# First products of the third token tile as two halves of 256 columns

## The chip, the cores and the metric

The kernel runs on one core of a Trainium2 chip. The metric is the device time of one execution in microseconds; lower is better. Three runs of the kernel before took 572.45 to 573.59 us, median 572.46.

## The reference

A decaying linear attention (2 sequences, 8 heads, 768 positions, head dimension 64) gives 1536 tokens of 512 features. They pass through two feed-forward layers, each 512 to 2048 to 512, the first with Mish, the second with SiLU:

```
x = attention(q, k, v, lam).reshape(1536, 512)
h = x @ w_in              # 1536 x 2048
x = (h * tanh(softplus(h))) @ w_out
h = x @ w2_in
out = (h * sigmoid(h)) @ w2_out
```

All is in float32.

## The kernel before

TensorE multiplies in float32r, one pass over four-byte operands. To keep float32 precision each operand is split in a high and a low part (`xh` and `xl` of the activations, `wh` and `wl` of the weights, `gh` and `gl` behind the nonlinearity), and each product is made of three: high by high, low by high, high by low.

The 1536 tokens are three tiles of 512 (t = 0, 1, 2). The 2048 hidden features of each layer are 16 blocks of 128; over both layers that makes 32 blocks n = 0 to 31, in eight groups of four. Group 0 runs for all three tiles during and just behind the attention (the first 92 us or so). From group 1 on, tiles 0 and 1 are taken together: the class `Block` (line 516) makes their first products by seven products of half size instead of eight (tiles `a`, `b`, `c`, `e`). Tile 2 goes alone, through `emit_h` (line 390).

`emit_h(t, n)` makes one block of h for one token tile: a PSUM bank `ph` of 128 features by 512 tokens, into which 12 matmuls accumulate: 4 slices `kk` of the 512 input features, times the three pairs of parts. Each has its own 128x128 weights; a float32r matmul loads them itself, and the trace shows that as a LDWEIGHTS record (engine PEld) and a MATMUL record (PE). Then `activate` (line 376) has ScalarE apply the nonlinearity twice, to `gh` and in place to `ph`, and DVE makes `gl` from the two (line 377). `emit_o` (line 413) makes the second products from `gh`, `gl`: 12 matmuls of 512 columns into four banks `po`, which over the four blocks of a group accumulate; DVE adds them to `acc` at the group's end (line 437).

The order of the work is written by hand: a list of steps for each group, issued in that order on every engine. In groups 2 to 7 the tail of the list interleaves the four `emit_h` of tile 2 with four `emit_o` of tile 1:

```
tail = [hs[0], os[4], hs[1], os[5], hs[2], os[6], hs[3], os[7]]
```

`hs[f]` is `emit_h(2, n0 + f)`. In group 3 the last two `hs` come together behind the last `os`. The second products of tile 2 (`fills`) follow in the next group. ScalarE, DVE and GpSimd split the weights of later groups meanwhile, and SyncE issues their loads from DRAM.

Of the kernel before, what the change touches and what calls it, by code (L numbers as in the profile page):

```python
# [17 lines left out]
def decay_attention_mish_silu_kernel(  # L18
# [8 lines left out]
    nc = tc.nc  # L27
    P = 128
# [6 lines left out]
    T = 512  # L35
    NB = NT // T
    CPB = T // C
    KD = DM // P
    NF = w1.shape[0]
    GF = 4  # L40
# [138 lines left out]
    def x_tile(key):  # L179
        if key not in xs:  # L180
            h = xp.tile([P, KD, T], F32R, tag="xh", name="xh")
            l = xp.tile([P, KD, T], F32R, tag="xl", name="xl")
            xs[key] = (h, l)
        return xs[key]
# [167 lines left out]
    def bank(name):  # L352
        nbank[0] += 1
        if len(late) > 2 and nbank[0] % 2:
            return late[2].tile([P, T], F32, tag="x", name=name)
        return ps_h.tile([P, T], F32, tag="h", name=name)
# [14 lines left out]
    def activate(ps, mm, t, n):  # L371

        gh, gl = [gp.tile([P, T], F32R, tag=tag, name=tag) for tag in ("gh", "gl")]
        gts[n, t] = (gh, gl)
        for to in (gh, ps):
            nc.scalar.activation(to, ps, AF.Mish if mm == 0 else AF.Silu)  # L376
        later.append(lambda: nc.vector.tensor_tensor(out=gl, in0=ps, in1=gh.bitcast(F32), op=ALU.subtract))  # L377

    def emit_h(t, n, first=False):
        mm = n // NF  # L380
        xt = x_tile(t)
        assert (n, 0) in ready and not any(key[0] == t for key, _ in rest)
        wi = wtiles[n, 0]
        ph = bank("ph")
        i = 0

        lst = (0, 1) if first else (1, 0)
        early = [(0, 0), lst[::-1]]
        for wsel, xsel, kk in [(*e, kk) for kk in range(KD) for e in early] + [(*lst, kk) for kk in range(KD)]:
            nc.tensor.matmul(  # L390
                ph, lhsT=wi[wsel][:, kk * P : (kk + 1) * P], rhs=xt[xsel][:, kk, :],
                start=(i == 0), stop=(i == 3 * KD - 1),
            )
            i += 1
        activate(ph, mm, t, n)

    def emit_o(t, n, first, last):
# [211 lines left out]
    for i, (t, f) in enumerate(steps):  # L609
        n = i + PH  # L610
# [11 lines left out]
        if i < LAG or n >= N:  # L622
            run_split(2)
        emit_h(t, f, f == 0)
        if n < N:
            if i < LAG:
# [22 lines left out]
    for g in range(1, 2 * NG):  # L649
# [4 lines left out]
        os = [(0, 0), (0, 1), (0, 2), (0, 3), (1, 1), (1, 0), (1, 3), (1, 2)]  # L654
        os = [o(t, f, i % 4 == 0, i % 4 == 3) for i, (t, f) in enumerate(os)]
        hs = [lambda n=n0 + f: emit_h(2, n) for f in range(GF)]
        sp = lambda fn, *a: lambda: fn(*a)
        nxt = [[lambda p=p: split_pair(p)] if p < NF else [] for p in (pa + 2, pa + 3)]
# [111 lines left out]
```

## Time and profile before

| | us |
|---|---|
| median of three runs | 572.46 |
| lowest and highest | 572.45, 573.59 |
| profiled execution | 572.03 |
| its span, first to last instruction | 570.3 |
| TensorE matmuls busy | 559.8 |
| TensorE weight loads busy | 454.9 |
| VectorE (DVE) busy | 314.4 |
| ScalarE (ACT) busy | 286.9 |
| GpSimd (POOL) busy | 163.1 |

A matmul is recorded from its start to the end that the profiler models for it; consecutive matmuls overlap, so a row's duration is longer than the time from one start to the next. Weight loads have an engine name of their own (PEld) and run beside matmuls. The tile names in a row are `out<-in`; numbers of buffers are left out. The mean granted clock of TensorE over the span is 0.998.

### The profile page before, as it was taken

How to read it: one execution, taken by the hardware profiler on the slowest of the kernel's cores; microseconds unless marked ns; L12 is line 12 of the kernel's file. 1: busy time of each engine (PE TensorE's matmuls, PEld its weight loads, DVE VectorE, ACT ScalarE, POOL GpSimd, SP SyncE). 2: the span in 40 equal slices, each digit the busy share in tenths (PEclk: the TensorE clock that was granted, in tenths of full speed). 3: DMA queues.
4: the chain of work that ended last, by engine and by line, in shares of the span. 5: the costliest groups of instructions: out<-in, count | busy, mean ns of one | idle time of the engine just before them, and what ended most of it. 6: DMA issues, size and time to landing. Idle time of an engine off the chain costs nothing.

```text
span 570.3 us, 7604 instructions
## 1 busy us (share of the span) xinstructions
PE 559.8 (98%) x2960; PEld 454.9 (80%) x2960; DVE 314.4 (55%) x458; ACT 286.9 (50%) x537; POOL 163.1 (29%) x139
## 2 busy tenths in 40 slices
PE   8999999999999999999999999999999999999996
PEld 5777777887787788888887788888888888888885
DVE  3675635684556675536669974434734654455231
ACT  2666442655454573354656874546543654355210
POOL 2564430322115123122362643211312212302000
PEclk9999999999999999999999999999999999999999
DMA  7984610123022132212211132212310322100103
GB/s 238 423 305 160 278 39 1 38 74 111 0 76 74 38 110 75 74 36 76 81 68 37 38 117 68 74 38 74 111 61 15 100 85 68 45 0 1 74 28 121
DMA packets 14072, 50.30 MB, mean 88 GB/s; under 512 B 1488, under 2 KB 2512, under 8 KB 12756
## 3 DMA queue, kind: packets, MB, share of 16 engines
q1 hardware_dynamic: 14036, 49.82, 24.8%
q8 instruction: 23, 0.38, 0.3%
q14 instruction: 13, 0.11, 0.1%
HBM read 46.66 MB, written 3.15 MB: 87 GB/s over the span
## 4 chain that ended last, share of the span: by engine, by line
PE 88%; DVE 3%; DMA 3%; ACT 2%; issue 2%; POOL 1%; SPq 0%; DVEq 0%; POOLq 0%; ACTq 0%
PE po L413 44%; PE ph L390 18%; PE b L516 9%; PE a L516 6%; PE c L516 3%; PE e L516 3%; DMA xslot<-x 2%; PE px L333 1%; PE s L292 1%; PE px L326 1%; DVE acc L437 1%; PE pc L312 1%; DVE acc L427 1%; ACT gh L376 1%; POOL qd L281 0%
## 5 line engine op out<-in xcount | busy, mean ns | idle before, releaser
L170 POOL TENSOR_TENSOR wl<-dec,wh 128x512 fp32r<-128x512 f32 x64 | 85.4, 1336 | 279.1 <-ACT wh L169 222.1
L413 PE MATMUL po<-gh,wh 128*128 128x512 f32 x192 | 75.9, 395 | 0.1
L413 PE MATMUL po<-gh,wl 128*128 128x512 f32 x192 | 74.9, 390 | 0.1
L413 PE MATMUL po<-wh,gh 128*128 128x512 f32 x192 | 74.8, 389 | 0.0
L413 PE MATMUL po<-wl,gh 128*128 128x512 f32 x192 | 74.7, 389 | 0.0
L413 PE MATMUL po<-wh,gl 128*128 128x512 f32 x192 | 74.7, 389 | 0.0
L377 DVE TENSOR_TENSOR gl<-ph,gh 128x512 fp32r<-128x512 f32 x40 | 27.5, 688 | 72.0 <-ACT ph L376 72.0
L376 ACT ACTIVATE gh<-ph 128x512 fp32r<-128x512 f32 x40 | 23.9, 598 | 81.0 <-PE ph L390 80.8
L390 PE MATMUL ph<-xh,wh 128*128 128x512 f32 x160 | 63.2, 395 | 0.7 <-ACT xh L340 0.7
L390 PE MATMUL ph<-xl,wh 128*128 128x512 f32 x160 | 60.8, 389 | 0.0
L125 DVE SCALAR_TENSOR_TENSOR dec<-dec,slot 128x512 uint32<-128x512 uint32 x64 | 50.7, 793 | 16.9 <-ACT slot L98 16.9
L437 DVE TENSOR_TENSOR acc<-po,acc 128x512 f32<-128x512 f32 x72 | 45.7, 685 | 23.7 <-PE po L413 23.7
L169 ACT CAST wh<-dec 128x512 fp32r<-128x512 f32 x64 | 39.5, 618 | 37.7 <-DVE dec L129 37.2
L170 POOL TENSOR_TENSOR tl<-t,th 128x512 fp32r<-128x512 f32 x28 | 37.8, 1358 | 61.8 <-ACT th L169 58.4
L129 DVE SCALAR_TENSOR_TENSOR dec<-slot,dec 128x512 uint32<-128x512 uint32 x64 | 50.6, 790 | 1.7
L413 PE MATMUL po<-gl,wh 128*128 128x512 f32 x192 | 51.4, 389 | 0.0
L390 PE MATMUL ph<-xh,wl 128*128 128x512 f32 x160 | 44.4, 390 | 0.0
L413 PEld LDWEIGHTS po<-gh,wh 128*128 128x128 f32 x192 | 36.0, 188 | 9.6 <-DVE acc L437 1.4
L97 ACT ACTIVATE dec<-slot 128x512 f32<-128x512 f32 x64 | 42.7, 667 | 0.2 <-DMA slot<-w 0.2
L98 ACT ACTIVATE slot<-slot 128x512 uint32<-128x512 uint32 x64 | 42.6, 666 | 0.0
L413 PEld LDWEIGHTS po<-wh,gh 128*128 128x128 f32 x192 | 36.0, 188 | 7.8 <-issue 0.3
L413 PEld LDWEIGHTS po<-gh,wl 128*128 128x128 f32 x192 | 36.0, 188 | 7.7 <-POOL wl L170 0.6
(117 smaller groups left out, 949.4 us busy)
## 6 DMA issues: line engine op xcount, KB each, us to landing
slot<-w SPq DMA_DIRECT2D x64, 512.0 KB, 3.6
xslot<-x SPq DMA_DIRECT2D x10, 1024.0 KB, 8.8
out<-acc SPq DMA_DIRECT2D x12, 256.0 KB, 2.1
xslot<-x SPq DMA_DIRECT2D x4, 512.0 KB, 4.2
dmask<-scr SPq DMA_DIRECT2D x2, 256.0 KB, 4.7
pw<-lam SPq DMA_DIRECT2D x1, 0.0 KB
scr<-pw SPq DMA_DIRECT2D x1, 8.0 KB
```

Source lines behind the costliest of these rows:

```text
L97: nc.scalar.activation(decs[n, i].bitcast(F32), high.bitcast(F32), AF.Copy, scale=2.0**-112)
L98: nc.scalar.activation(low, low, AF.Copy, scale=TOP3, bias=2.0**-21 - 0.5)
L125: nc.vector.scalar_tensor_tensor(out=d, in0=d, scalar=3, in1=low, op0=ALU.logical_shift_left, op1=ALU.bitwise_or)
L129: nc.vector.scalar_tensor_tensor(out=d, in0=high, scalar=0x80000000, in1=d, op0=ALU.bitwise_and, op1=ALU.bitwise_or)
L169: nc.scalar.copy(hi, f)
L170: nc.gpsimd.tensor_tensor(out=lo, in0=f, in1=hi.bitcast(F32), op=ALU.subtract)
L376: nc.scalar.activation(to, ps, AF.Mish if mm == 0 else AF.Silu)
L377: later.append(lambda: nc.vector.tensor_tensor(out=gl, in0=ps, in1=gh.bitcast(F32), op=ALU.subtract))
L390: nc.tensor.matmul(ph, lhsT=wi[wsel][:, kk * P : (kk + 1) * P], rhs=xt[xsel][:, kk, :], start=(i == 0), stop=(i == 3 * KD - 1),)
L413: nc.tensor.matmul(po[t][j], lhsT=lhsT, rhs=rhs, start=(first and wsel + gsel == 0), stop=(last and gsel == 1))
L437: nc.vector.tensor_tensor(out=acc[:, j, :], in0=po[t][j], in1=acc[:, j, :], op=ALU.add)
L516: nc.tensor.matmul(self.b[dst], lhsT=w[ws][:, kk * P : (kk + 1) * P], rhs=x[xx][:, kk, :], start=(start and i == 0), stop=(i == 5), skip_g ...
```

## The change

For t = 2 and n >= 8 (groups 2 to 7, 24 calls of `emit_h`) the 12 matmuls of 512 columns become two rounds of 12 with 256 columns each, into the left and then the right half of the same bank. Only the first matmul of the first round carries the start flag, which marks the bank as empty; the first of the second round finds its columns unwritten and overwrites them. `activate` follows both rounds, as before. All other calls keep one round of 512 columns.

```
-        i = 0
-
         lst = (0, 1) if first else (1, 0)
         early = [(0, 0), lst[::-1]]
-        for wsel, xsel, kk in [(*e, kk) for kk in range(KD) for e in early] + [(*lst, kk) for kk in range(KD)]:
-            nc.tensor.matmul(
-                ph, lhsT=wi[wsel][:, kk * P : (kk + 1) * P], rhs=xt[xsel][:, kk, :],
-                start=(i == 0), stop=(i == 3 * KD - 1),
-            )
-            i += 1
+        order = [(*e, kk) for kk in range(KD) for e in early] + [(*lst, kk) for kk in range(KD)]
+        width = T // 2 if t == 2 and n >= 2 * GF else T
+        for c in range(0, T, width):
+            for i, (wsel, xsel, kk) in enumerate(order):
+                nc.tensor.matmul(
+                    ph[:, c : c + width], lhsT=wi[wsel][:, kk * P : (kk + 1) * P],
+                    rhs=xt[xsel][:, kk, c : c + width], start=(c == 0 and i == 0), stop=(i == 3 * KD - 1),
+                    skip_group_check=True,
+                )
         activate(ph, mm, t, n)
```

On TensorE, the end of the last of the 24 pieces and what follows it, before (`wh` and `wl` are the two parts of the weights, `x4` stands for four matmuls over `kk`; a row has the weight load in it):

```order
L390 MATMUL ph<-xh,wh_4152 128x512
L390 MATMUL ph<-xl,wh_4152 128x512
L390 MATMUL ph<-xh,wl_4153 128x512 x4
L413 MATMUL po<-wh_4347,gh 128x512
L413 MATMUL po<-wl_4348,gh 128x512
L413 MATMUL po<-wh_4347,gl 128x512
```

The same place of TensorE's order now, at the seam between the two rounds (the line numbers are one higher):

```order
L391 MATMUL ph<-xh,wh_4380 128x256
L391 MATMUL ph<-xl,wh_4380 128x256
L391 MATMUL ph<-xh,wl_4381 128x256 x4
L391 MATMUL ph<-xh,wh_4380 128x256
L391 MATMUL ph<-xl,wh_4380 128x256
L391 MATMUL ph<-xh,wh_4380 128x256
```

Where `po` came, the same weights now come a second time for the other 256 columns, 12 matmuls more, and `po` follows these. On ScalarE, DVE, GpSimd and SyncE the instructions stand in the same order in both programs.

## Rows read from the trace of the kernel before

**Rows 1.** The page: its head, TensorE's busy time, the chain by engine and line.

```profile
span 570.3 us, 7604 instructions
...
PE 559.8 (98%) x2960; PEld 454.9 (80%) x2960; DVE 314.4 (55%) x458; ACT 286.9 (50%) x537; POOL 163.1 (29%) x139
...
PE 88%; DVE 3%; DMA 3%; ACT 2%; issue 2%; POOL 1%; SPq 0%; DVEq 0%; POOLq 0%; ACTq 0%
PE po L413 44%; PE ph L390 18%; PE b L516 9%; PE a L516 6%; PE c L516 3%; PE e L516 3%; DMA xslot<-x 2%; PE px L333 1%; PE s L292 1%; PE px L326 1%; DVE acc L437 1%; PE pc L312 1%; DVE acc L427 1%; ACT gh L376 1%; POOL qd L281 0%
```

**Rows 2.** Busy time by stretch, bf16 start, groups 2 and 7; columns in the first row.

```profile
core 0: us, PE busy (x) PEld busy (x) DVE busy (x) ACT busy (x) POOL busy (x), PEclk, DMA share, GB/s
7.00:8.20 1.20, 1.20 (x8) 0.54 (x6) 0.00 (x0) 0.00 (x0) 0.00 (x0) 1.00 0.90 293
196.00:268.00 72.00, 71.81 (x317) 59.16 (x316) 41.06 (x61) 39.41 (x73) 19.74 (x15) 1.00 0.24 81
510.00:560.00 50.00, 50.00 (x221) 41.21 (x220) 18.36 (x29) 14.47 (x27) 4.23 (x3) 1.00 0.12 43
```

**Rows 3.** Groups by line and shape: count, busy us, mean ns, idle before.

```profile
L390 PE MATMUL ph<-xl,wh 128*128 128x512 f32 x160 | 60.8, 389 | 0.0
...
L390 PEld LDWEIGHTS ph<-xl,wh 128*128 128x128 f32 x160 | 30.0, 188 | 6.1
```

**Rows 4.** Timeline, TensorE matmuls of the last piece: start us, duration us, what.

```profile
548.76 0.39 PE L390 MATMUL ph<-xh,wh 128*128 128x512 f32 x1
548.99 0.39 PE L390 MATMUL ph<-xl,wh 128*128 128x512 f32 x1
...
551.48 0.39 PE L413 MATMUL po<-wh,gh 128*128 128x512 f32 x1
```

**Rows 5.** Timeline, weight loads of the same piece.

```profile
548.99 0.19 PEld L390 LDWEIGHTS ph<-xh,wh 128*128 128x128 f32 x1
```

**Rows 6.** Waits from 92 to 570 us: total us, times, longest.

```profile
ACT gh L376 <- PE ph L390: 70.2, 23, 7.1
...
PEld e L516 <- DVE gl L377: 2.1, 3, 0.9
PEld b L516 <- ACT b L535: 1.5, 2, 0.8
PEld po L413 <- DVE acc L437: 1.4, 4, 0.5
```

**Rows 7.** Timeline behind a stall of TensorE: matmuls, and (PEld) weight loads.

```profile
175.63 0.50 PE L413 MATMUL po<-gh,wh 128*128 128x512 f32 x1
175.98 0.39 PE L413 MATMUL po<-gh,wl 128*128 128x512 f32 x1
...
175.63 0.19 PEld L413 LDWEIGHTS po<-gh,wh 128*128 128x128 f32 x1 [0.53 <-DVE acc L437]
175.74 0.19 PEld L413 LDWEIGHTS po<-gh,wl 128*128 128x128 f32 x1
```

**Rows 8.** Loads of 128 columns in the attention: by shape; timeline of one chunk's matmuls.

```profile
L292 PEld LDWEIGHTS s<-xslot 64*128 64x128 f32 x192 | 11.7, 187 | 3.8 <-issue 1.4 <-DVE dec L129 1.1 <-DMA xslot<-x 0.9
...
24.75 0.83 PE L292 MATMUL s<-xslot 64*128 64x128 f32 x11
...
25.30 0.27 PE L292 MATMUL s<-xslot 64*128 64x128 f32 x1
```

**Rows 9.** The chain in order of time: start us, us, what.

```profile
78.13 2.95 PE ph L390 x12
...
101.18 2.72 PE ph L390 x12
...
563.39 2.73 DVE acc L437 x4
```

**Rows 10.** Timeline, bf16 matmuls of 512 columns at the same clock.

```profile
7.21 1.24 PE L203 MATMUL warm<-zeros 128*64 128x512 bf16 x5
```

## The prediction

> **What bounds the kernel now.** I read the page's head and its chain first, then the busy time by stretch, then the timeline of one of the 24 pieces that the change touches, and last the places where TensorE stood still. The head says TensorE is busy for 559.8 of 570.3 us, and the chain that ended last is 88% TensorE, with the first products (`ph`) at 18% of the span [rows 1]. The reader is to see there that no other engine sets the end. The busy share alone proves little, because a matmul of 512 columns is recorded for 389 ns or more [rows 3] and the records overlap. So the stretches are read with the timeline: in the stretches of groups 2 and 7 TensorE is busy for all but 0.19 us, at a granted clock of 1.00, which is the 2.4 GHz level [rows 2].
>
> The timeline of the last of the 24 pieces gives the number on which all else rests. Its first matmul starts at 548.76 and the first matmul of the next step at 551.48: 12 matmuls in 2.72 us, 226.7 ns from one start to the next [rows 4]. The chain gives the same 2.72 us for 12 [rows 9]. At 2.4 GHz, 512 columns are 512 / 2.4 = 213.3 ns, so each matmul costs **13.3 ns over its columns**. Each is accompanied by one weight load; the load for the third matmul starts at 548.99, together with the second matmul [rows 4, 5], and so on for the others. So a load lies beside the matmul before it, and has 227 ns to get done. What ended waits there: ScalarE waits for TensorE's `ph` (70.2 us in 23 waits), not the reverse, while TensorE's weight loads waited for DVE and ScalarE only 2.1 + 1.5 + 1.4 us in all, at other steps [rows 6]. So what the 24 pieces gain or lose, the end gains or loses.
>
> **The change, part by part.** It removes 24 x 12 = 288 matmuls of 512 columns with their 288 weight loads, and adds 24 x 24 = 576 of 256 columns with 576 loads. The columns streamed are the same: 2 x 256 for every 512. The instructions of ScalarE, DVE, GpSimd and the DMA queues stand in the order of before; `activate` still comes after the last of all 24 matmuls, so nothing is handed on earlier, and no wait is added. Of the twelve loads that are done twice, none reads other data. What the trace doesn't show is a matmul of 256 columns with a 128x128 load, so its start-to-start time has to be bounded.
>
> From below, by the load. After a stall it can be seen alone: the load starts at 175.63 with TensorE idle, its matmul is recorded for 0.50 us where an undisturbed one has 0.39, and the second load starts at 175.74 [rows 7]. A load thus takes about 0.11 us until its matmul really streams and the next load may start. The 188 ns recorded for a load [rows 3] is therefore not what it occupies. The attention stage agrees: there loads of 128 columns, recorded at 187 ns each, go two at a time, and a matmul and the five pairs behind it start within 0.83 - 0.27 = 0.56 us, 0.112 us for each pair [rows 8]. So a half can't go faster than about 112 ns. Its own columns take 256 / 2.4 = 106.7 ns. So the load would be the limit if the columns were all; it fits under the half, but hardly.
>
> From above, by the nearest row: a half that costs what a whole one does now, 226.7 ns, if the start-to-start time were one per instruction and not per column.
>
> Between these I take 106.7 + 13.3 = **120 ns**, the cost over the columns as fixed for each matmul with its load. A reason to take it as fixed: bf16 matmuls of the same 512 columns at the same clock go every (1.24 - 0.38) / 4 = 0.215 us [rows 2, 10], so the 13.3 ns isn't the streaming of 512 columns as such; what is different here is a four-byte operand and, with each instruction, a load of 128 four-byte columns. And the surplus moves with how the load lies to the matmul: 12 matmuls right behind a stall take 2.95 us in place of 2.72 [rows 9], 0.23 more, of which the bare load is only 0.11. A surplus that belongs to the meeting of load and matmul is paid once per load, and the loads double.
>
> The rule for the gap in the Trainium skill ("TensorE: Matmul & The Clock Gate", section "Back-to-back issue gap") says N / 2.4 + 2.5 ns: by it the change costs 288 x 2.5 = 0.7 us. The bf16 row bears it out within a nanosecond or so; the float32r rows of this kernel don't, with 13.3 in place of 2.5.
>
> The sum: a piece takes 24 x 120 = 2880 ns instead of 12 x 226.7 = 2720, so 160 ns more; 24 pieces give 24 x 0.160 = **3.84 us**. All of it is on TensorE, and on the path. Nothing hides it: the chain's pieces of `ph` lie back to back with those of `po`. Little is given back later either: the waits of TensorE that other engines could catch up on sum to the 5.0 us named above, and most of those engines wait for TensorE's own product just before. The end (four additions on DVE and their stores [rows 9]) moves with TensorE. The profiled execution took 572.03 us (span 570.3 and 1.7 around it): 572.03 + 3.84 = 575.87. The median of the three runs is 572.46, 0.43 above the profiled execution, so I forecast **576.3 us**, 0.67% slower. What a measurement of this kernel can tell from no change is about 0.2%, 1.1 us.
>
> **Rivals.**
>
> *Not slower: the surplus goes by the column.* 226.7 / 213.3 is 17/16; if the operand arrives at 16 columns in the time of 17, a half costs 113.3 ns, just above the 112 of the load, and a piece takes 24 x 113.3 = 2720 ns, as now: 572.5. With the load alone as limit (112 ns) it would be 24 x (2688 - 2720) = -0.8 us, 571.7. For it: the ratio comes out even, and the operand is twice as wide as in bf16. Against it: the surplus isn't constant behind stalls. Place: every half; it decides for anything under about 115 ns per half, (115 x 24 - 2720) x 24 = 1.0 us. The Trainium skill's rule of the gap would end on this side too, at 573.2. I give this side 24%.
>
> *Slower than forecast: load and matmul never lock in.* At 120 ns a load of 112 has 8 ns of slack where it now has 115. Where load and matmul meet badly, as behind a stall, 12 matmuls cost 2.95 - 2.72 - 0.11 = 0.12 us more, 10 ns each [rows 7, 9]. If that lasts, a half takes 130 ns: 24 x (3120 - 2720) = +9.6 us, 582.1. For it: the slack; against it: away from stalls 12 matmuls take 2.72 us [rows 4, 9]. 11%.
>
> *Much slower: the load isn't hidden.* If a matmul had to wait for the recorded end of its load, 188 ns after its start, a half would cost at least 188 ns: 24 x (4512 - 2720) = +43.0 us, 615.5. For it: the recorded load [rows 3]; against it: rows 7 and 8, in which the next thing starts after 110 to 112 ns. 3%. The same page of the Trainium skill (section "The mechanism", on packing small matmuls) says that loads overlap running matmuls only where the row group differs. By that a half would take 107 + 112 = 219 ns and the change would cost 24 x (5256 - 2720) = 60.9 us; rows 4 and 5 speak against it, since full-array loads start beside full-array matmuls and these still follow each other in 227 and not 213 + 112 = 325 ns.
>
> *Faster: the stalls close.* The halves give DVE and ScalarE a little more time per piece, and the 5.0 us of waits of TensorE [rows 6] shrink. If halves went at 112 ns and half of those waits went, the sum would be -0.8 - 2.5 = -3.3 us, 569.2. But none of those waits lies in a piece with `ph`. 4%.
>
> That the change doesn't do what it says can be left out: the program has the 256-wide rows in all 24 places.
>
> **How the numbers follow.** Fixed surplus: 58%; by the column: 24%; no lock: 11%; not hidden: 3%; faster: 4%. The predicted time is that of the likeliest, 576.3; its own range, for 118 to 122 ns per half, is 575.1 to 577.5. Since the other side holds 24% the range reaches down to it, and up to about 127 ns per half (24 x (3048 - 2720) = +7.9 us): 571.5 to 580.5. Slower by over 0.2%: 58 + 11 + 3 = 72%; within 0.2%: 24%; faster: 4%.
>
> **What would show it.** In the timeline of any of the 24 pieces: 24 matmul starts 120 ns apart, 2.88 us for the piece; the loads still recorded at about 188 ns, each starting with the matmul before its own. The other groups of matmuls (512 columns) stay at 226.7 ns, and the waits of rows 6 change by less than a microsecond. If the piece takes 2.72 us, the surplus goes by the column and the forecast is wrong; if it takes over 3.0 us, the load has become the limit or never locks in. If the piece comes out at 2.88 and the time doesn't rise, then the loss was paid back at a wait of rows 6.

## The result and the profile after

The kernel after took 575.98 us (median of 5 runs, 574.80 to 576.27) against 572.57 for the kernel before (5 runs): ratio 1.0052, 95% interval 1.0041 to 1.0064. The medians differ by 3.41 us, and the interval makes it 2.3 to 3.7; the forecast was 3.84, a little above that.

The page after, its head, TensorE's busy time and the chain by engine and line (a line number of `ph` or `po` is one higher than in [rows 1]):

```profile
span 574.2 us, 8191 instructions
...
PE 564.1 (98%) x3248; PEld 470.3 (82%) x3248; DVE 313.6 (55%) x458; ACT 286.9 (50%) x537; POOL 164.6 (29%) x139
...
PE 91%; DMA 3%; ACT 2%; issue 1%; POOL 1%; DVE 1%; SPq 0%; POOLq 0%; DVEq 0%; ACTq 0%
PE po L414 45%; PE ph L391 19%; PE b L517 9%; PE a L517 6%; PE c L517 3%; PE e L517 3%; DMA xslot<-x 2%; PE px L333 1%; PE s L292 1%; PE px L326 1%; PE pc L312 1%; DVE acc L438 1%; ACT gh L376 1%; POOL qd L281 0%; DMA scr<-pw 0%
```

The matmuls went up by 288, as the diff says; the other engines have the same counts as in [rows 1]. Those counts leave out semaphore instructions: the head went from 7604 to 8191, which is 288 matmuls, 288 loads and 11 semaphore instructions that DVE has more than before (128 and not 117); they matter at the end of this document. The bound is the same. The stretches of [rows 2], after:

```profile
core 0: us, PE busy (x) PEld busy (x) DVE busy (x) ACT busy (x) POOL busy (x), PEclk, DMA share, GB/s
...
196.00:268.00 72.00, 71.81 (x362) 61.10 (x361) 41.53 (x62) 38.65 (x72) 19.72 (x15) 1.00 0.24 76
510.00:560.00 50.00, 50.00 (x266) 43.17 (x266) 20.04 (x31) 18.46 (x34) 5.53 (x4) 1.00 0.06 22
```

In these stretches the clock and TensorE's busy time have not changed; there are more instructions in the same time. Now the last of the 24 pieces, to be held against [rows 4, 5]: first TensorE's matmuls with what stands ahead of the piece and behind it, then two weight loads.

```profile
550.92 0.40 PE L414 MATMUL po<-wh,gh 128*128 128x512 f32 x1
551.15 0.40 PE L414 MATMUL po<-wl,gh 128*128 128x512 f32 x1
551.39 0.39 PE L414 MATMUL po<-wh,gl 128*128 128x512 f32 x1
...
553.66 0.28 PE L391 MATMUL ph<-xh,wh 128*128 128x256 f32 x1
553.78 0.28 PE L391 MATMUL ph<-xl,wh 128*128 128x256 f32 x1
553.90 0.28 PE L391 MATMUL ph<-xh,wh 128*128 128x256 f32 x1
554.02 0.28 PE L391 MATMUL ph<-xl,wh 128*128 128x256 f32 x1
...
556.54 0.40 PE L414 MATMUL po<-wh,gh 128*128 128x512 f32 x1
...
553.90 0.19 PEld L391 LDWEIGHTS ph<-xl,wh 128*128 128x128 f32 x1
554.02 0.19 PEld L391 LDWEIGHTS ph<-xh,wh 128*128 128x128 f32 x1
```

The halves start 0.12 us apart, and 24 of them take 556.54 - 553.66 = 2.88 us instead of 2.72 (to three digits 2.872: the first step is 0.113, the others 0.120). The loads are still recorded at 0.19 us, and each starts with the matmul before its own. Behind a piece something stands that the prediction had not priced: the next matmuls, of 512 columns, come after 0.23 and 0.24 us, and the 12 of them take 553.66 - 550.92 = 2.74 us. From the chain of both kernels, the period of piece and `po` is 5.62 us now against 24 x 0.2267 = 5.44: 0.18 per piece, of which 0.152 in the piece and 0.027 behind it.

The chain after, two pieces in order of time (start us, us, what):

```profile
548.21 2.87 PE ph L391 x24
553.83 2.87 PE ph L391 x24
```

The waits after, from 92 us on, against [rows 6]:

```profile
ACT gh L376 <- PE ph L391: 80.2, 26, 7.2
...
PEld e L517 <- DVE gl L377: 2.1, 3, 0.9
PEld po L414 <- DVE acc L438: 1.4, 4, 0.5
PEld b L517 <- ACT b L536: 1.1, 2, 0.7
```

ScalarE waits longer for `ph`. One wait of TensorE got shorter: that of the weight loads for ScalarE's copy of `b`, from 1.5 to 1.1 us. The matmul at the start of group 4 had stood still for it by 0.39 us; first the row before, then the row after, which has no wait:

```profile
313.26 0.73 PE L516 MATMUL b<-sh,th 128*128 128x512 f32 x2 [0.39 <-ACT b L535]
...
315.46 0.73 PE L517 MATMUL b<-sh,th 128*128 128x512 f32 x2
```

### The profile page after: what moved, and what is told of

Read it like the earlier page. It is cut to its first block, busy times and chain, and to the rows that moved or that the text cites. A ratio compares the mean times of both kernels' runs of the same rounds, so it can differ in the third digit from the quotient of the medians.

```text
span 574.2 us, 8191 instructions
## 1 busy us (share of the span) xinstructions
PE 564.1 (98%) x3248; PEld 470.3 (82%) x3248; DVE 313.6 (55%) x458; ACT 286.9 (50%) x537; POOL 164.6 (29%) x139
## 4 chain that ended last, share of the span: by engine, by line
PE 91%; DMA 3%; ACT 2%; issue 1%; POOL 1%; DVE 1%; SPq 0%; POOLq 0%; DVEq 0%; ACTq 0%
PE po L414 45%; PE ph L391 19%; PE b L517 9%; PE a L517 6%; PE c L517 3%; PE e L517 3%; DMA xslot<-x 2%; PE px L333 1%; PE s L292 1%; PE px L326 1%; PE pc L312 1%; DVE acc L438 1%; ACT gh L376 1%; POOL qd L281 0%; DMA scr<-pw 0%
## 5 line engine op out<-in xcount | busy, mean ns | idle before, releaser
L391 PE MATMUL ph<-xh,wh 128*128 128x256 f32 (+1 forms) x256 | 73.9, 313 | 0.7 <-ACT xh L340 0.7
L391 PE MATMUL ph<-xl,wh 128*128 128x256 f32 (+1 forms) x256 | 71.7, 310 | 0.0
L391 PEld LDWEIGHTS ph<-xh,wh 128*128 128x128 f32 x256 | 48.7, 190 | 5.0 <-ACT xh L340 0.9
L391 PEld LDWEIGHTS ph<-xl,wh 128*128 128x128 f32 x256 | 48.9, 191 | 3.2
L391 PE MATMUL ph<-xh,wl 128*128 128x256 f32 (+1 forms) x256 | 49.6, 310 | 0.0
```

Of the source, the lines that this page charges most:

```text
L391: nc.tensor.matmul(ph[:, c : c + width], lhsT=wi[wsel][:, kk * P : (kk + 1) * P], rhs=xt[xsel][:, kk, c : c + width], start=(c == 0 and i ...
```

## The experiments

For each, the time is read where runs were compared, and, in the profiled execution, the **stretch** from the start of the last attention product to the start of the last matmul. It leaves out the attention, which ends anywhere from 92.5 to 95.8 us in these traces with the same instructions (in some of them TensorE's clock differs early on: from 15.0 to 18.5 us the granted clock was 0.51 in the second trace of before, the 1.2 GHz level for nearly all of it, and 1.00, the 2.4 GHz level, in the first and the third; what else moves that end is not shown), and the **tail** behind the start of the last matmul. The last column is the ratio of the times times the median of before in that comparison.

| kernel | pieces changed | last attention product, us | last matmul, us | stretch, us | over before | tail, us | time over before, us |
|---|---|---|---|---|---|---|---|
| before | 0 | 92.52 | 565.01 | 472.49 | | 5.25 | |
| before, second and third time | 0 | 94.22, 93.02 | 566.70, 565.52 | 472.49, 472.50 | 0 | 5.25, 5.25 | |
| after | 24 | 93.69 | 570.06 | 476.38 | +3.89 | 4.15 | +3.0 (2.3 to 3.7) |
| after, second time | 24 | 93.43 | 569.78 | 476.35 | +3.86 | 4.15 | +3.0 (2.0 to 4.1) |
| groups 2 to 4 | 12 | 95.44 | 569.69 | 474.25 | +1.76 | 4.14 | +0.7 (0.1 to 1.4) |
| groups 5 to 7 | 12 | 95.42 | 570.02 | 474.60 | +2.11 | 4.14 | +1.1 (0.4 to 1.8) |
| group 3 | 4 | 92.91 | 565.73 | 472.83 | +0.33 | 4.15 | |
| cut at 384 | 24 | 94.95 | 584.71 | 489.76 | +17.27 | 4.14 | +16.2 (15.3 to 17.2) |
| halves in pairs | 24 | 94.49 | 570.83 | 476.33 | +3.84 | 4.14 | +3.3 (2.6 to 4.1) |
| before, fetch moved | 0 | 95.83 | 568.29 | 472.46 | -0.03 | 4.15 | -1.4 (-2.0 to -0.9) |

**A table of matmuls.** What is the 13.3 ns, and where does the load take over?

```
+    xw, xr = x_tile(0)[0], x_tile(1)[0]          # behind the last emit_o of the kernel before
+    series = [("r", w, c) for w in (128, 64) for c in (512, 384, 256, 192, 128, 64)]
+    series += [("b", 128, c) for c in (512, 256, 128)] + [("r", 128, 512)]
+    for k, (kind, w, c) in enumerate(series):
+        ...
+        for i in range(24):
+            nc.tensor.matmul(probe[0:w, 0:c], lhsT=lhsT, rhs=rhs, start=True, stop=True)
```

> The kernel before, with a table of matmuls added behind its last work: series of 24 matmuls each, on data that lie ready, every matmul with a weight load of its own. float32r with 128 weight columns and 512, 384, 256, 192, 128, 64 columns; the same with 64 weight columns; bf16 with 128 weight columns and 512, 256, 128; float32r 128 x 512 again. What is read is the time from one start to the next within a series. Theory (a fixed surplus of 13.3 ns per float32r matmul, and a load that hides as long as it takes no more than 112 ns): 226.7, 173.3 and 120 ns for 512, 384 and 256 columns, and from 192 down the load sets 112 ns. First rival (the surplus goes by the column, 17/16): 226.7, 170, and the 120 ns at 256 is then already the load, so 192, 128 and 64 columns take 120 as well. Second rival (the surplus is there only because load and matmul meet): with 64 weight columns it falls to half, 220, 167, 113 ns. If it belongs to the four-byte operand alone, 64 weight columns change nothing at 512 columns and bf16 goes at 216, 109 and 107 to 112 ns.

The timeline of this kernel, one row from inside each of six series (start us, us from the first start to the last end, what, count; `128*64` means 64 weight columns):

```profile
568.17 4.70 PE L736 MATMUL r128x<-xh 128*128 128x512 f32 x20
577.81 2.32 PE L736 MATMUL r128x<-xh 128*128 128x256 f32 x18
583.28 2.17 PE L736 MATMUL r128x<-xh 128*128 128x128 f32 x18
588.66 4.53 PE L736 MATMUL r64x<-xh 128*64 128x512 f32 x19
598.33 1.86 PE L736 MATMUL r64x<-xh 128*64 128x256 f32 x15
605.98 4.26 PE L736 MATMUL b128x<-xb 128*128 128x512 bf16 x19
```

Less the duration of the last matmul, and over the steps, these are (4.70 - 0.39) / 19 = 0.227 us, (2.32 - 0.28) / 17 = 0.120, (2.17 - 0.27) / 17 = 0.112, (4.53 - 0.39) / 18 = 0.230, (1.86 - 0.28) / 14 = 0.113 and (4.26 - 0.38) / 18 = 0.216. From the single starts, the mean of the last eight steps in ns:

| | 512 | 384 | 256 | 192 | 128 | 64 columns |
|---|---|---|---|---|---|---|
| float32r, 128 weight columns | 226.6 | 173.4 | 120.0 | 111.6 | 111.6 | 111.8 |
| float32r, 64 weight columns | 230.1 | 173.4 | 113.4 | 88.5 | 60.0 | 58.3 |
| bf16, 128 weight columns | 215.9 | | 109.3 | | 55.9 | |

With 128 weight columns the theory holds: 512, 384 and 256 columns each take their columns plus 13.3 ns, and below that the load sets 111.6 ns. So the 120 ns at 256 isn't the load's limit, 8 ns lie between. The first rival is out (384 columns take 173.4 ns and not 170, and the load's limit is 111.6 ns and not 120). bf16 at the same clock pays 2.5 ns. With 64 weight columns the answer is mixed: the surplus halves at 256 columns (6.7 ns), as the second rival says, and doesn't at 384 and 512.

**The second table: the width of the load.**

```
+    series = [(w, 512, 0) for w in (128, 96, 64, 32)] + [(w, 256, 0) for w in (128, 96, 64, 32)]
+    series += [(128, c, 0) for c in (448, 320, 240)] + [(128, 512, 1), (64, 512, 1), (128, 256, 1)]
+    for w, c, same in series:
+        ...
+        for i in range(48):
+            kk = 0 if same else i % KD
+            nc.tensor.matmul(probe[0:w, 0:c], lhsT=xw[:, kk, 0:w], rhs=xr[:, kk, 0:c], start=True, stop=True)
```

> The kernel before with a second table behind its last work: series of 48 float32r matmuls, 512 and 256 columns against 128, 96, 64 and 32 weight columns, 448, 320 and 240 columns against 128 weight columns, and three series in which all matmuls use the same weights and data. It is to tell what the 13.3 ns hang on, after the first table had 120.0 ns for 256 columns with 128 weight columns and 113.4 with 64. Theory (a matmul streams one eighth slower while a load of weights is read beside it, 107 ns for 128 columns): at 256 columns 120, 116.7, 113.3 and 110 ns for 128, 96, 64 and 32 weight columns, at 512 columns 226.7, 223.3, 220, 216.7; 448 columns 200, 320 columns 146.7, 240 columns 113.3. Rival (13.3 ns per matmul, whatever the load): 120 and 226.7 ns in all of them. The first table speaks against the theory at 512 columns with 64 weight columns (230 ns, unsteady): if that comes again, neither explains it. Same weights and data: no difference in the theory; if the addresses matter, these series are steadier or shorter.

The timeline of this kernel, from inside four series, read as above:

```profile
565.62 10.14 PE L732 MATMUL varied<-xh 128*128 128x512 f32 x44
598.82 10.36 PE L732 MATMUL varied<-xh 128*32 128x512 f32 x44
610.32 4.72 PE L732 MATMUL varied<-xh 128*128 128x256 f32 x38
626.83 4.36 PE L732 MATMUL varied<-xh 128*32 128x256 f32 x37
```

From the single starts, here the mean of the last 24 steps, because in some of these series the steps repeat in a pattern that eight steps don't cover evenly:

| weight columns | 128 | 96 | 64 | 32 |
|---|---|---|---|---|
| 512 columns, ns | 226.7 | 230.0 | 230.0 | 231.7 |
| 256 columns, ns | 120.0 | 116.1 | 113.3 | 113.3 |

At 256 columns the surplus falls with the load from 13 to 9 to 7 ns and then stays. At 512 a narrower load makes the matmul slower, not faster; the steps there repeat in a pattern (224, 227, 234, 230, 236, 229 ns with 64 weight columns), and do so with the same weights and data each time. So neither the theory (an eighth slower beside a load) nor the rival (13.3 ns whatever the load) holds outside 128 weight columns. With those, 320 columns take 146.7 ns (13.3 over), 240 take 112.0, and 448 take 202.8 (16.1 over), so even there the 13.3 ns isn't a law for every width. With fewer weight columns the result has fewer rows too (`probe[0:w]`), so the table doesn't tell the load's width from the result's height. What makes the surplus stays open.

**Half the pieces, groups 2 to 4.**

```
-        width = T // 2 if t == 2 and n >= 2 * GF else T
+        width = T // 2 if t == 2 and 2 * GF <= n < 5 * GF else T
```

> The change in groups 2 to 4 alone, 12 of the 24 pieces. Theory (TensorE bound, a fixed price for each piece): the trace after has each piece 0.152 us longer and 0.027 us more behind it, so 12 x 0.18 = 2.15 us, less the 0.4 us of a wait at the fifth group that closed in the trace after, which lies in this half: +1.8 us, ratio 1.003. Rival (the loss is not made by the pieces but once, or later in the program): +3.4 us as with all 24, or nothing.

The stretch grew by 1.76 us, as the theory has it. The time did not: its ratio is 1.0013 (1.0001 to 1.0025), +0.7 us and at most 1.4. As a forecast of the time the 1.8 missed; the runs on the tail, below, say why.

**The other half, groups 5 to 7.**

```
-        width = T // 2 if t == 2 and n >= 2 * GF else T
+        width = T // 2 if t == 2 and n >= 5 * GF else T
```

> The change in groups 5 to 7 alone, the other 12 pieces. Theory: 12 x 0.18 = 2.16 us, and the wait of 0.39 us at the start of group 4 stays, since nothing ahead of it has changed: the stretch from the last attention product to the last matmul grows from 472.49 to 474.65 us, and the time by +2.2 us, ratio 1.0038. Rival (the price of a piece depends on how many there are, as the half dose of groups 2 to 4 with its ratio of 1.0013 could be read): about +0.8 us in the time, and less than 2 us in the stretch.

The stretch is 474.60, forecast 474.65. The two halves add up there, 1.76 + 2.11 = 3.87 of the 3.89: the price is per piece, and the rival is out. The time has the ratio 1.0020 (1.0007 to 1.0032), again below the forecast of 1.0038. At the start of group 4 the wait stands as before (waits from 300 to 320 us):

```profile
PEld b L517 <- ACT b L536: 0.8, 1, 0.8
PE b L517 <- ACT b L536: 0.4, 1, 0.4
```

**Group 3 alone.**

```
-        width = T // 2 if t == 2 and n >= 2 * GF else T
+        width = T // 2 if t == 2 and n // GF == 3 else T
```

> The change in group 3 alone, 4 of the 24 pieces, read in the trace: the stretch from the last attention product to the last matmul. Theory (the wait of TensorE for ScalarE's copy of b at the start of group 4 closes because the pieces just ahead of it, those of group 3, give ScalarE time): 4 x 0.152 + 3 x 0.027 - 0.39 = +0.30 us, 472.79, with no wait there. Rival (it closes only with group 2 changed as well, or by chance): +0.69 us, 473.18, and the wait of some 0.4 us is there.

The stretch is 472.83, forecast 472.79. The same stretch of time, 300 to 320 us, now has only one row of the two:

```profile
PEld b L517 <- ACT b L536: 0.4, 1, 0.4
```

The pieces of group 3, just ahead, give ScalarE the time to have the copy ready; the wait of the matmul is gone, and that of the load is half. The rival is out: the matmul's wait is gone in every trace with group 3 changed, and stands, at 0.3 or 0.4 us, in every one without.

**Cut at 384.**

```
+        cuts = (0, 384, T) if t == 2 and n >= 2 * GF else (0, T)
+        for c, end in zip(cuts, cuts[1:]):
+            width = end - c
```

> The 24 pieces cut at column 384 in place of 256: a round of 12 matmuls of 384 columns, then one of 128. Theory (fixed surplus of 13.3 ns, load of 112 ns): 12 x 173.3 + 12 x 112 = 3424 ns for a piece in place of 2720, so 24 x 0.70 = +16.9 us, about 589.5. If the load's own limit is 120 ns, 12 x (173.3 + 120) = 3520 ns and +19.2 us, 591.8. If the limit were the columns alone, without the load (66.7 ns for 128 columns), a piece would cost 2880 as with halves, +4.3 us.

590.33 us, ratio 1.0283 (1.0267 to 1.0299): +16.2 us, and 17.27 in the stretch. The 19.2 of a 120 ns load and the columns alone are out by either figure. The theory's 16.9 lies in the interval of the time and 0.4 below the stretch. It is near with other terms than the sum has: a piece costs 3.392 and not 3.424 us, each leaves some 0.08 us behind it, and the wait at the start of group 4 closes. The timeline of the last piece, at the start of its narrow round:

```profile
569.89 0.22 PE L392 MATMUL ph<-xh,wh 128*128 128x128 f32 x1
569.95 0.27 PE L392 MATMUL ph<-xl,wh 128*128 128x128 f32 x1
570.06 0.27 PE L392 MATMUL ph<-xh,wh 128*128 128x128 f32 x1
570.17 0.28 PE L392 MATMUL ph<-xl,wh 128*128 128x128 f32 x1
...
571.18 0.45 PE L415 MATMUL po<-wh,gh 128*128 128x512 f32 x1
```

Half as many columns as in a half cost 0.11 us, nearly what a half costs: here the load is the bound.

**The halves in pairs.**

```
-        for c in range(0, T, width):
-            for i, (wsel, xsel, kk) in enumerate(order):
+        for i, (wsel, xsel, kk) in enumerate(order):
+            for c in range(0, T, width):
```

> The change with its two loops exchanged: the left and the right half of each product stand one behind the other, with the same weights, instead of in two rounds. Theory (each float32r matmul loads its weights, same or not, and pays 13.3 ns): 120 ns per half as after the change, the same time, about 576. Rival (the chip leaves out a load of weights that are in the array, or the surplus comes from the exchange of weights): every second half takes 107 to 109 ns, a piece 12 x (120 + 108) = 2736 ns, and the time is that of before, 572.9.

577.46 us, ratio 1.0058 (1.0046 to 1.0071); the stretch is 476.33, as with the change. The timeline of its last piece has pairs with the same weights, 0.24 us from pair to pair:

```profile
554.92 0.40 PE L391 MATMUL ph<-xh,wh 128*128 128x256 f32 x2
555.16 0.40 PE L391 MATMUL ph<-xl,wh 128*128 128x256 f32 x2
555.40 0.40 PE L391 MATMUL ph<-xh,wh 128*128 128x256 f32 x2
```

The trace has a load for each half, as after the change: weights that are in the array already are loaded and paid for again.

**The tail.** By now every time had come out below its stretch, by 0.5 to 1.1 us, and among the kernels without a table the trace of before alone had the longer tail. So the kernels before and after ran again, unchanged, before twice.

> The kernel before once more, for its tail: in its first trace the last matmul starts 5.25 us ahead of the end, in all traces of changed kernels 4.14 or 4.15, and every comparison of times came out 0.5 to 1.1 us below the growth of the stretch. Theory (the last store's landing varies from one execution to the next): the stretch is 472.49 again, the tail 4.14 us in this one or the next. Rival (the tail of before is 1.1 us longer always, for instance by where its last store falls): 5.25 us here as well, and the time then gains 1.1 us less than the stretch by any of the changes.

> The kernel before a third time, with the same two expectations: a tail of 4.14 us (theory) or of 5.25 us (rival), a stretch of 472.49 us in both; and the end of the attention, 92.5 us in the first trace, somewhere up to 95.4 us if it varies by execution, at 92.5 if it doesn't.

> The changed kernel once more: stretch 476.38 us, tail 4.15 us if that belongs to this kernel, up to 5.25 us if it varies by execution; attention over somewhere between 92.5 and 95.4 us.

My theory fell: the tail is 5.25 us in all three traces of before and 4.15 in both of after, to 0.01 us. It belongs to the kernel. (The end of the attention does vary: 92.5, 94.2 and 93.0 us in before.) The waits of SyncE's queue name the place, what ends the program after the last store; first in before, second time:

```profile
SPq L766 <- DMA out<-acc: 2.7, 3, 1.7
```

and in after, second time (total us, times, longest):

```profile
SPq L767 <- DMA out<-acc: 1.6, 3, 0.6
```

The last wait for a store is 1.7 us long and not 0.6. Among the packets of the trace there is one more in that place in before: an instruction packet of 8192 bytes, queue 14, which begins 1.82 us behind the last addition and takes 309 ns; the last two packets of the store begin at 2.13, just as it ends, and 2.21 us, where the store of after is over by 1.72. In after, queue 14's last instruction packet comes at 552.2 us, 19 us ahead of the last addition's end. The matmuls' own instructions are on another queue (8: 23 packets in before, 25 in after). Of the engines besides TensorE only DVE has another number of instructions: 128 semaphore instructions instead of 117. The two tables of matmuls, which have more instructions on TensorE and as many on DVE as before, keep the packet at 1.82 us and the wait at 1.7 us. So the number of TensorE's instructions doesn't move it. If the number of DVE's does, any few instructions there should:

```
+    nudge = const.tile([P, 1], F32, name="nudge")
...
         activate(ph, mm, t, n)
+        if t == 2 and n >= 2 * GF and n % 2:
+            nc.vector.memset(nudge, 0.0)
```

> The kernel before, with 12 memsets of one column on DVE (of a tile that nothing reads), one behind every second of the 24 pieces; TensorE's work is unchanged. In all three traces of the kernel before an instruction packet of 8192 bytes is fetched 1.82 us behind the last addition on DVE, among the packets of the last store, and the last two packets of that store come behind it; in the changed kernels, which have 4 to 11 more semaphore instructions on DVE, the packet was fetched some 10 to 15 us earlier, and the tail is 4.15 us instead of 5.25. Theory (the fetch belongs to DVE's instructions, and makes the tail longer): 12 more DVE instructions move it, the tail is 4.15 us, the stretch 472.49 us as before, and the time 1.1 us lower, ratio 0.9981. Rival (the tail hangs on something else in the changed kernels): tail 5.25 us, the time of before or a little more.

572.14 us, ratio 0.9975 (0.9966 to 0.9984), tail 4.15, stretch 472.46; the last instruction packet of queue 14 comes at 546.3 us. The waits of SyncE's queue:

```profile
SPq L769 <- DMA out<-acc: 1.6, 3, 0.6
```

What the theory forecast came: 12 more instructions on DVE moved the packet, and the tail went with it. In all 13 traces the two go together: the packet lies either 1.82 us behind the last addition, and the last store is waited for 1.7 us (before three times, and the two tables), or 13 to 23 us ahead of the addition's end, and the wait is 0.6 us (the eight with more instructions on DVE; in the changed kernels that is 15 to 21 us earlier, and not the 10 to 15 of the expectation). This version is 0.25% faster than before, by 1.4 us (0.9 to 2.0). Of the 1.1 us the packets show 0.53, by which the store ends later with the fetch among its packets; how the rest comes about stays open.

## Why the prediction was right, and where it was not

**The bound** was right: TensorE sets the end, with the halves on the path, and every changed group moves the stretch.

**The price of a half** was forecast at 120 ns, between 112 and 226.7; it is 2.872 / 24 = 119.7. The lower bound was good as well: 112 from [rows 7, 8], and 111.6 in the table and in the narrow round of the cut at 384.

**The sum** came out at 3.84 forecast and 3.89 in the stretch, but with terms that cancel, and that is luck. A piece costs 0.152 and not 0.160, because its first step is 0.113. Each piece that isn't followed by another one also leaves 0.027 us behind it, where 512 columns take up again; this was not in the sum. And the wait of TensorE at the start of group 4 gives 0.39 back, which the sentence "Little is given back later either" had left at nothing. 24 x 0.152 + 23 x 0.027 - 0.39 = 3.88. The 5.0 us of that sentence were waits of weight loads; at that place the load had waited 0.8 us and the matmul lost 0.39.

**What went unseen** is the end. That the end "moves with TensorE" is the sentence that failed. The tail gets 1.10 us shorter; the change adds 11 semaphore instructions on DVE, an instruction packet leaves the last store's way, and the run with 12 memsets shows that this alone is enough. That makes 3.89 - 1.10 = 2.79 us, and the time rose by 3.0 (2.3 to 3.7 by the ratio; the medians differ by 3.41). The other comparisons fit in the same way: 0.66 for groups 2 to 4 (measured 0.7), 1.01 for groups 5 to 7 (1.1), 2.74 for the pairs (3.3), 16.17 for the cut at 384 (16.2). In the trace before, the last store's wait of 1.7 us and the packets show this; the rows of the tail had been read for their additions alone. So the forecast of the change, 3.84 us, lies above what the time shows, and that the forecast of the time, 576.3, is only 0.3 us from the median of 575.98 is in part luck: from one execution to another the attention's end alone moves by more than that. (The range's upper end of 580.5 is 572.46 + 7.9 = 580.4 by its own sum.)

**The reason for a fixed surplus** is the weak step. "A surplus that belongs to the meeting of load and matmul is paid once per load" holds in the table at 256 columns, where it shrinks with the load (120, 116, 113 ns for 128, 96 and 64 weight columns). At 512 columns it does not: 226.7 with the widest load, 231.7 with the narrowest. The value was taken from the right rows, all with 128 weight columns, and is paid per matmul there; the mechanism given for it is not shown.

**The rivals.** By the column: refuted by the 120 ns of the pieces (113.3 expected), though 113.3 is just what 64 or 32 weight columns give. Load and matmul never lock in: inside the pieces they do at the second step; what there is of unsteady steps comes behind the pieces, 0.027 us each and not 10 ns per half. The load isn't hidden: refuted by the same pieces and by 111.6 ns steps of 128 columns. Faster by closing stalls: the mechanism exists, one wait of 0.39 us, and is a tenth of the price.

**The rule of the gap** in the Trainium skill ("TensorE: Matmul & The Clock Gate", section "Back-to-back issue gap") is met to 0.1 ns by the bf16 series of the table (215.9, 109.3 and 55.9 ns for 512, 256 and 128 columns) and by none of float32r: 120.0 where it has 109.2. The sentence in the section "The mechanism" of the same page of the Trainium skill, that loads overlap running matmuls only where the row group differs, doesn't hold here as it stands: full-array loads lie beside full-array matmuls at 120 ns a step, which is less than 106.7 of columns plus 111.6 of load.

## What to carry to other kernels

Where TensorE is the bound, count a split by its start-to-start time in the trace less the columns: here the difference, 13.3 ns, was paid again for each half that a matmul was cut into. Measure it at the width that is wanted, since with other widths and narrower loads it was 7 to 18 ns. Then look for the load by itself, behind a stall, since it was the floor for pieces of 192 columns and fewer, and its recorded duration (188 ns) is not what it occupies (112). Read small changes in the stretch that they touch, and then ask what the whole time adds: here a wait just behind gave 0.39 us back, and a tail that got shorter as an instruction fetch moved out of the last store gave 1.10, more than a quarter of the price.

## What was not expected of the hardware

- A float32r matmul of 512 columns gets slower with a narrower load: 226.7 ns with 128 weight columns, 230 to 232 with 96, 64 or 32.
- bf16 loads of 128 columns hide under 128-column matmuls of 55.9 ns, where float32r needs 111.6.
- With an instruction fetch of 8192 bytes among the packets of the last store the end came 1.10 us later, in all three traces of before; 12 tiny instructions on DVE moved the fetch away and the end forward. 0.53 us of it is seen in the store's packets.
- The change from 256 back to 512 columns costs some 0.027 us, spread over the next few matmuls.
